# Beacon attention followed by a gated feed-forward block: queries in blocks that line up with the key tiles, whole-batch DMA transposes, and the fourth result pair turned by DMA

## The chip, the cores and the metric

The kernel runs on one core of a Trainium2 chip. The metric is the device time of one execution in microseconds (us). Where a profile is read, PE is TensorE (matmuls; PEld its weight loads), DVE is VectorE, ACT is ScalarE, POOL is GpSimd and SP is SyncE, which here only issues DMAs. A "q" behind an engine (SPq) is its instruction queue.

## The reference: what is computed

```python
# q, k, v: (8, 8, 576, 64); beacon_k, beacon_v: (8, 8, 16, 64)
k_all = np.concatenate([beacon_k, k], axis=2)          # 592 keys
v_all = np.concatenate([beacon_v, v], axis=2)
scores = scale * np.matmul(q, k_all.transpose(0, 1, 3, 2))
causal[:, Nb:] = np.triu(np.ones((S, S), dtype=bool), k=1)   # beacons are seen by all
scores = np.where(causal, -1e9, scores)
a = softmax(scores)
attn = np.matmul(a, v_all)                             # (8, 8, 576, 64)
x = attn.transpose(0, 2, 1, 3).reshape(4608, 512)
g, val = x @ w_gate, x @ w_val                         # (4608, 1536)
out = (gelu(g) * val) @ w_out                          # (4608, 512), float32
```

## The kernel before

**Two interleaved stages.** There are 8 batches of 576 tokens (attention) and 9 chunks of 512 tokens (feed-forward). In pass `b` of the main loop (L561) the attention of batch `b` is computed head pair by head pair (4 pairs of 2 heads), and between its pieces stand the output matmuls of chunk `b-1`, in portions `o(n)` of n matmuls (48 in all for a chunk). Then the gate and value matmuls of chunk `b` follow (`gv_mms`, `gate_val`): 12 tiles of 128 hidden columns, each with 4 steps `kk` over the 512 model columns. Step `kk` reads the attention result of head pair `kk`. So a pass has an attention stage of some 20 us and a gate and value stage of some 19 us. The order of all instructions is written out by hand (`keep`).

**Attention of a pair.** Scores are computed transposed, keys on partitions: five key tiles of 128, 128, 128, 128 and 80 rows (16 beacons, then 576 keys). Key tile t only meets the queries from `S_LO[t]` on (0, 112, 240, 368, 496), so the query blocks have 112, 128, 128, 128 and 80 (96 with the last) queries and are shifted by 16 against the key tiles. `CHUNKS` packs the score matmuls of a pair into four PSUM pieces of 512, 480, 464 and 208 columns for each head (`scores`, `score_mms`). Two heads use the two halves of TensorE's rows. ACT takes the exponential into `expT`, POOL masks the diagonal blocks (`masks`, L298), PE multiplies with v (`attend`; a column of ones gives the sum), and DVE divides (`normalize`: L334, L336) into `y_sb`.

**Queries and keys are needed transposed** (`qkT`, one buffer: pair, q or k, 640 columns). For batches 0 and 1 TensorE transposes them. For batches 2 to 7 POOL loads q and k (L108), with a conversion from float32 to bf16, into a ring of two buffers, two batches ahead. In the pass before they are used, SP issues ten DMA transposes (`transpose_dma`, L238): five token tiles, q and k in turn, each with 4 blocks of at most 128x128.

**Results are needed transposed** too (`xT_sb`, the feed-forward input). For b of 1 to 7 pairs 0, 1 and 2 are turned by two DMA transposes each on SP's queue (`turn_dma`, L368: the first 112 rows, then four tiles). Pair 3 is turned by TensorE: five transposes (`turn`, `tr`, L180) into PSUM in the midst of the output matmuls, and a DVE copy (`put`, L386). The first two tiles of gate and value run their steps in the order pair 0, 3, 1, 2.

**What stands on the queues at the start of the gate and value stage** (L622 to L630): SP stores what is left of the outputs; POOL waits in `hold` (L378) until pair 2 has landed in `xT_sb`, and then issues the loads of v for batch b+1 and of q and k for batch b+2; SP issues the ten transposes for batch b+1. Each chunk has four output stores of 128 rows. Two are issued by ACT in the attention stage (L582, L597) and two by SP, one at L609 and one at L623.

Of the kernel before, what the change touches and what calls it, by code (L numbers as in the profile page):

```python
# [7 lines left out]
P = 128  # L8
B, H, S, NB, D = 8, 8, 576, 16, 64
SK = S + NB  # L10
N_TOK = B * S
# [9 lines left out]

S_LO = [0, 112, 240, 368, 496]
KROWS = [128, 128, 128, 128, 80]
DIAG = [112, 128, 128, 128, 80]


CHUNKS = [
    [(0, 0, 512, 0)],
    [(0, 512, 64, 0), (2, 240, 336, 64), (4, 496, 80, 400)],
    [(1, 112, 464, 0)],  # L30
    [(3, 368, 208, 0)],
]
CHUNK_W = [512, 480, 464, 208]
CHUNK_OFF = [0, 512, 992, 1456]
EXP_W = 1664

EXP_OFF = [0, 992, 576, 1456, 912]
DV = D + 1

Q_N = [128, 128, 128, 128, 80]  # L40
QK_SCALE = 0.125
# [10 lines left out]
def kernel(  # L52
# [16 lines left out]
    ring = ctx.enter_context(tc.tile_pool(name="ring", bufs=1))  # L69
    npool = ctx.enter_context(tc.tile_pool(name="npool", bufs=4))  # L70
    fpool = ctx.enter_context(tc.tile_pool(name="fpool", bufs=3))
    hpool = ctx.enter_context(tc.tile_pool(name="hpool", bufs=2))
# [12 lines left out]
    wo_sb = const.tile([P, F_TILES, D_MODEL], BF16, name="wo_sb", tag="wo_sb")  # L85
    xT_sb = const.tile([P, NPAIR, N_TOK + P - Q_N[4]], BF16, name="xT_sb", tag="xT_sb")

    exp_ring = ring.tile([P, NPAIR, 2, EXP_W + P - Q_N[4]], BF16, name="expT", tag="expT")
    nc.vector.memset(exp_ring[:, :, :, EXP_W:], 0.0)

# [10 lines left out]

    qkT = ring.tile([P, NPAIR, 2, 640], BF16, name="qkT", tag="qkT")
    nc.vector.memset(qkT[:, :, 1, SK:640], 0.0)

    neg = const.tile([P, 256], BF16, name="neg", tag="neg")
# [6 lines left out]
    def qk6_of(b):  # L112
        if b not in qk6:
            qk6[b] = (
                hpool.tile([P, 2, H, 6 * D], BF16, name="qk6", tag="hT_sb"),
                npool.tile([NB, H, D], BF16, name="kb", tag="kb"),
            )
        return qk6[b]
# [12 lines left out]
    def key_loads(src, beacon, dst, b):  # L131
        parts = [
            (dst[0:NB, 0, :, :], beacon[b].rearrange("h t d -> t h d")),
            (dst[NB:P, 0, :, :], src[b, :, 0:112, :].rearrange("h p d -> p h d")),
        ]
        for j in range(1, 5):
            n = KROWS[j]
            r0 = 112 + (j - 1) * P
            parts.append((dst[0:n, j, :, :], src[b, :, r0 : r0 + n, :].rearrange("h p d -> p h d")))
        return [lambda o=o, i=i: dma(o, i) for o, i in parts]  # L140

    def qk_loads(b):
        q_sb, k_sb = q_ring[b % NRING], k_ring[b % NRING]
        parts = []
        for j in range(5):
            n = P if j < 4 else 64
            parts.append(
                (q_sb[0:n, j, :, :], q[b, :, j * P : j * P + n, :].rearrange("h p d -> p h d"))
            )
        return [lambda o=o, i=i: dma(o, i) for o, i in parts] + key_loads(k, beacon_k, k_sb, b)  # L150

# [81 lines left out]
    def transpose_dma(b):  # L233
        q_sb, k_sb = q_ring[b % NRING], k_ring[b % NRING]
        for j in range(5):
            for w, src, n, c in ((0, q_sb, P if j < 4 else 64, NB), (1, k_sb, P if j < 4 else 80, 0)):
                keep(
                    nc.sync.dma_start_transpose(  # L238
                        out=qkT[:, :, w, c + j * P : c + j * P + n],
                        in_=src[0:n, j, :, :].rearrange("p h d -> p (h d)"),  # L240
                    )
                )

    def scores(b, *parts):
# [17 lines left out]
    def score_mms(b, m, c, s_ps):  # L262
        for t, s_lo, w, col in CHUNKS[c]:
            diag = b == 0 and s_lo == S_LO[t]
            for hi in range(2):
                r = slice(64 * hi, 64 * hi + 64)
                mm(
                    s_ps[:, hi, col : col + w],
                    qkT[r, m, 1, t * P : (t + 1) * P],
                    qkT[r, m, 0, NB + s_lo : NB + s_lo + w],  # L270
                    True,
                    not diag,
                    skip_group_check=True,
                )
            if diag:
                base, n = (NB if t == 0 else 0), DIAG[t]
                for k0, width in ((0, min(n, 64 - base)), (64, n)):
                    for hi in range(2):
                        r = slice(64 * hi, 64 * hi + 64)
                        c0 = 64 + 64 * hi - k0  # L280
                        mm(
                            s_ps[:, hi, col : col + width],
                            eye[r, c0 : c0 + P],
                            neg[r, c0 + base : c0 + base + width],
                            False,
                            k0 == 64,
                            skip_group_check=True,
                        )

    def masks(b, m, c):  # L290
        expT = exp_ring[:, m, :, :]
        for t, s_lo, _, _ in CHUNKS[c]:
            if s_lo != S_LO[t]:
                continue
            n = DIAG[t]
            d = expT[0 : KROWS[t], :, EXP_OFF[t] : EXP_OFF[t] + n]
            keep(
                nc.gpsimd.affine_select(  # L298
                    out=d,
                    in_=d,  # L300
                    pattern=[[0, 2], [1, n]],
                    compare_op=ALU.is_ge,
                    fill=0.0,
                    base=NB if t == 0 else 0,
                    channel_multiplier=-1,
                )
            )

    x_of = {}

    def attend(b, m, hi, x_ps):
        expT, v_sb = exp_ring[:, m, :, :], v_ring[b % NRING]
        for j in range(5):
            for t in range(j + 1):
                e0 = EXP_OFF[t] + S_LO[j] - S_LO[t]
                mm(
# [10 lines left out]
    def normalize(b, m, x_ps, h0, h1):  # L327
        i = b * NPAIR + m
        if h0 == 0:
            y_of[i] = npool.tile([P, 5, 2, D], BF16, name="y_sb", tag="y_sb")  # L330
        r_sb = npool.tile([P, 2, 5, 1], FP32, name="r_sb", tag="r_sb")
# [18 lines left out]
    def av_head(b, m, hi, pool, tag):  # L350
        x = pool.tile([P, 1, 512], FP32, name="x_ps", tag=tag)
        attend(b, m, hi, x[:, 0, :])
        normalize(b, m, x, hi, hi + 1)

    def turn(b, m, pool=None, tag="t"):
        y_sb = y_of[b * NPAIR + m].rearrange("p j e d -> p j (e d)")
        y_ps = (pool or psum_t).tile([P, 1024], BF16, name="y_ps", tag=tag)
        y_of[b * NPAIR + m] = y_ps
        for j in range(5):
            n = Q_N[j] if j else S_LO[1]  # L360
            tr(y_ps[:, S_LO[j] : S_LO[j] + n], y_sb[0:n, j, :])

    def turn_dma(b, m):
        y_sb = y_of.pop(b * NPAIR + m)
        n0 = b * S
        for n, j0, j1, q0 in ((S_LO[1], 0, 1, 0), (P, 1, 5, S_LO[1])):
            keep(
                nc.sync.dma_start_transpose(  # L368
                    out=xT_sb[:, m, n0 + q0 : n0 + q0 + n * (j1 - j0)].rearrange("p (j n) -> p j n", n=n),
                    in_=y_sb[0:n, j0:j1, :, :].rearrange("p j e d -> p (j e d)"),  # L370
                )
            )

    hold_sb = const.tile([P, 2], BF16, name="hold_sb", tag="hold_sb")
# [5 lines left out]
    def put(b, m, by_act=False):  # L380
        y_ps = y_of.pop(b * NPAIR + m)
        out_ap = xT_sb[:, m, b * S : (b + 1) * S]
        if by_act:
            act(out_ap, y_ps[:, 0:S], ACT.Copy)
        else:
            keep(nc.vector.tensor_copy(out_ap, y_ps[:, 0:S]))  # L386

# [173 lines left out]
    for b in range(B):  # L561
# [6 lines left out]
        if b:  # L568
# [12 lines left out]
            scores(b, (1, 2))  # L581
            store(nc.scalar)  # L582
            ahead(2)
# [12 lines left out]
            scores(b, (3, 0))  # L596
            store(nc.scalar)  # L597
            av_head(b, 1, 0, psum_o, "o")
# [8 lines left out]
            av(b, 3)  # L607
            o(7)
            store(nc.sync)  # L609
            turn(b, 3)  # L610
            put(b, 3)
            o(4)
            keep(nc.scalar.preload_act_table_set(SET_GELU))
            for kk in (0, 3, 1, 2):
                for fi in range(2):
                    gv_mms(b, fi, kk, last=kk == 2)
        for fi in range(F_TILES):
# [4 lines left out]
            if fi == 0:  # L622
                store(nc.sync)  # L623
                if b and b + 1 < B:
                    hold(b, 2)
                    load_v(b + 1)
                if b and b + 2 < B:
                    load_qk(b + 2)
                if 2 <= b + 1 < B:
                    transpose_dma(b + 1)  # L630
    for fi in range(F_TILES):
        gate_val(N_CHUNKS - 1, fi)
        out_mms(N_CHUNKS - 2, 4 * fi, 4 * fi + 4)
# [37 lines left out]
```

## Time and profile before

Six runs of the kernel have a median of 369.24 us (368.76 to 370.71).

| what | value |
|---|---|
| the profiled execution's own time | 370.71 us |
| its span in the profile | 369.0 us |
| PE busy | 358.9 us, 97% of the span, 3018 matmuls |
| DVE, ACT, POOL busy | 152.5 (41%), 188.2 (51%), 160.5 us (43%) |
| gate and value matmuls (both kinds, 795 recorded) | 110.9 + 110.9 us |
| output matmuls | 101.7 us |
| score matmuls x384; matmuls with v x960 | 34.1 us; 37.1 us |
| POOL's loads and SP's transposes and stores, packets | 104848 on q0; 48000 on q1 |

The profile's page gives busy time of each engine, the chain of work that ended last, and groups of instructions. Durations of single matmuls are latencies (they overlap); what one costs in a row of matmuls is the distance from start to start. Of SP the profile shows only issues; the time of a transfer is that from the issue to the landing of its last byte's semaphore. Some matmul records are missing: about every 10.8 us one start is left out, which looks like a gap of 0.05 us and is none.

### The profile page before, as it was taken

How to read it: one execution, taken by the hardware profiler on the slowest of the kernel's cores; microseconds unless marked ns; L12 is line 12 of the kernel's file. 1: busy time of each engine (PE TensorE's matmuls, PEld its weight loads, DVE VectorE, ACT ScalarE, POOL GpSimd, SP SyncE). 2: the span in 40 equal slices, each digit the busy share in tenths (PEclk: the TensorE clock that was granted, in tenths of full speed). 3: DMA queues.
4: the chain of work that ended last, by engine and by line, in shares of the span. 5: the costliest groups of instructions: out<-in, count | busy, mean ns of one | idle time of the engine just before them, and what ended most of it. 6: DMA issues, size and time to landing. Idle time of an engine off the chain costs nothing.

```text
span 369.0 us, 7507 instructions
## 1 busy us (share of the span) xinstructions
PE 358.9 (97%) x3018; PEld 184.2 (50%) x3061; DVE 152.5 (41%) x277; ACT 188.2 (51%) x243; POOL 160.5 (43%) x288
## 2 busy tenths in 40 slices
PE   7899999999999999999999999999999999999996
PEld 7674546444554446444644454445544464444443
DVE  3454545433344335343533254434444253334332
ACT  3873489136933594339723792369344953331210
POOL 8934478383548252953476353936230430000000
PEclk9899999999999999999999999999999999999999
DMA  7999999799249954999399925992395051000112
GB/s 107 176 203 204 193 121 120 135 147 136 74 111 147 135 61 107 153 143 91 69 159 134 121 63 123 156 138 74 105 132 56 31 81 58 0 2 29 57 37 108
DMA packets 154900, 39.65 MB, mean 107 GB/s; under 512 B 141424, under 2 KB 150384, under 8 KB 154864
## 3 DMA queue, kind: packets, MB, share of 16 engines
q0 software_dynamic: 104848, 19.11, 67.9%
q1 hardware_dynamic: 48000, 16.38, 26.2%
q10 hardware_dynamic: 2016, 3.67, 3.1%
q8 instruction: 24, 0.39, 0.4%
q14 instruction: 12, 0.10, 0.1%
HBM read 38.27 MB, written 9.44 MB: 129 GB/s over the span
## 4 chain that ended last, share of the span: by engine, by line
PE 76%; DMA 12%; SPq 4%; POOL 2%; issue 2%; DVE 2%; ACT 1%; POOLq 0%; DVEq 0%
PE gv_ps L172 32%; PE o_ps L172 23%; PE x_ps L172 9%; PE s_ps L172 8%; DMA qkT<-k_sb 7%; DMA q_sb<-in_q_dram 4%; SPq L238 3%; PE t_ps L180 2%; POOL v_sb L108 2%; DMA xT_sb<-y_sb 1%; PE w_ps L172 1%; PE v_ps L172 1%; ACT expT L175 1%; PE g_ps L172 1%; PE y_ps L180 1%
## 5 line engine op out<-in xcount | busy, mean ns | idle before, releaser
L175 ACT ACTIVATE ge_sb<-gv_ps 128x512 bf16<-128x512 f32 x101 | 59.4, 597 | 144.5 <-PE gv_ps L172 142.6
L427 DVE TENSOR_TENSOR hT_sb<-gv_ps,ge_sb 128x512 bf16<-128x512 f32 x101 | 69.1, 691 | 115.5 <-ACT ge_sb L175 113.1
L172 PE MATMUL gv_ps<-xT_sb,wg_sb 128*128 128x512 bf16 x394 | 110.9, 379 | 0.5
L172 PE MATMUL gv_ps<-xT_sb,wv_sb 128*128 128x512 bf16 x401 | 110.9, 379 | 0.1
L175 ACT ACTIVATE expT<-s_ps 128x960 bf16<-128x960 f32 (+3 forms) x112 | 99.8, 966 | 9.3 <-PE s_ps L172 8.4
L172 PE MATMUL o_ps<-wo_sb,hT_sb 128*128 128x512 bf16 (+2 forms) x415 | 101.7, 373 | 1.4 <-issue 0.2
L298 POOL TENSOR_SCALAR_AFFINE_SELECT expT<-expT 128x256 bf16<-128x256 bf16 (+2 forms) x140 | 51.5, 385 | 67.6 <-ACT expT L175 66.8
L172 PEld LDWEIGHTS <-wv_sb 128*128 128x128 bf16 x432 | 42.3, 98 | 50.4
L172 PEld LDWEIGHTS <-wg_sb 128*128 128x128 bf16 x432 | 42.0, 98 | 50.4 <-DMA xT_sb<-y_sb 0.6
L172 PEld LDWEIGHTS <-hT_sb 128*128 128x128 bf16 x444 | 38.9, 98 | 42.3 <-DVE y_sb L336 3.1
L172 PEld LDWEIGHTS <-expT 128*128 128x128 bf16 (+1 forms) x960 | 33.5, 97 | 10.8 <-DVE y_sb L336 4.1
L172 PE MATMUL s_ps<-qkT 64*128 64x512 bf16 (+5 forms) x384 | 34.1, 285 | 3.5 <-DVE qkT L221 1.0
L172 PE MATMUL x_ps<-v_sb,expT 128*128 128x65 bf16 (+1 forms) x960 | 37.1, 193 | 0.0
L446 DVE COPY o_sb<-o_ps 128x512 f32<-128x512 f32 (+2 forms) x37 | 25.0, 676 | 27.3 <-PE o_ps L172 26.2
L108 POOL DMA_DIRECT2D v_sb<-in_v_dram x40 | 33.6, 858 | 5.9 <-DMA wv_sb<-in_moe_w_val_dram 1.7
L108 POOL DMA_DIRECT2D k_sb<-in_k_dram x30 | 25.2, 843 | 17.8 <-DMA q_sb<-in_q_dram 13.7
L336 DVE TENSOR_TENSOR y_sb<-x_ps,r_sb 128x320 bf16<-128x320 f32 (+1 forms) x47 | 28.8, 612 | 1.6
L334 DVE RECIPROCAL r_sb<-x_ps 128x5 f32<-128x5 f32 (+1 forms) x47 | 9.6, 204 | 47.0 <-PE x_ps L172 47.0
L108 POOL DMA_DIRECT2D q_sb<-in_q_dram x30 | 25.3, 887 | 3.5 <-DMA wo_sb<-in_moe_w_out_dram 3.5
L172 PEld LDWEIGHTS <-qkT 64*128 64x128 bf16 x384 | 14.5, 95 | 19.6 <-issue 12.3
L378 POOL COPY hold_sb<-xT_sb 128x2 bf16<-128x2 bf16 x6 | 1.1, 186 | 33.3 <-DMA xT_sb<-y_sb 33.3
L569 ACT ACT_TABLE_LOAD x7 | 9.0, 1283 | 0.1
(49 smaller groups left out, 122.4 us busy)
## 6 DMA issues: line engine op xcount, KB each, us to landing
out_dram<-o_sb SPq DMA_DIRECT2D x21, 256.0 KB, 2.2
out_dram<-o_sb ACTq DMA_DIRECT2D x14, 256.0 KB, 2.7
v_sb<-in_v_dram POOLq DMA_DIRECT2D x24, 128.0 KB, 6.3
q_sb<-in_q_dram POOLq DMA_DIRECT2D x24, 128.0 KB, 8.1
k_sb<-in_k_dram POOLq DMA_DIRECT2D x18, 128.0 KB, 7.8
wo_sb<-in_moe_w_out_dram POOLq DMA_DIRECT2D x3, 512.0 KB, 14.4
wg_sb<-in_moe_w_gate_dram POOLq DMA_DIRECT2D x2, 512.0 KB, 11.3
wv_sb<-in_moe_w_val_dram POOLq DMA_DIRECT2D x2, 512.0 KB, 12.6
```

Source lines behind the costliest of these rows:

```text
L108: keep(nc.gpsimd.dma_start(out=out_ap, in_=in_ap))
L172: keep(nc.tensor.matmul(out_ap, lhsT, rhs, start=start, stop=stop, **kw))
L175: keep(nc.scalar.activation(out_ap, in_ap, func, **kw))
L180: keep(nc.tensor.transpose(out_ap, in_ap, ident[0:n, 0:n]))
L238: nc.sync.dma_start_transpose(out=qkT[:, :, w, c + j * P : c + j * P + n], in_=src[0:n, j, :, :].rearrange("p h d -> p (h d)"),)
L298: nc.gpsimd.affine_select(out=d, in_=d, pattern=[[0, 2], [1, n]], compare_op=ALU.is_ge, fill=0.0, base=NB if t == 0 else 0, channel_multip ...
L334: keep(nc.vector.reciprocal(r, x[:, :, :, D:DV]))
L336: nc.vector.tensor_tensor(out=y_of[i][:, :, h0:h1, :].rearrange("p j b d -> p b j d"), in0=x[:, :, :, 0:D], in1=r.to_broadcast([P, h1 - h0 ...
L378: keep(nc.gpsimd.tensor_copy(hold_sb, x[:, 0 : S : S - 1]))
L427: nc.vector.tensor_tensor(out=h_of[ci][:, fi, :], in0=gv_of.pop((ci, fi))[1], in1=ge_sb, op=ALU.mult)
L446: keep(nc.vector.tensor_copy(o_sb[:, ti, c0:c1], o_ps))
L569: keep(nc.scalar.preload_act_table_set(SET_EXP))
```

## The change

1. **Query blocks line up with key tiles.** 16 empty columns stand ahead of the queries (as the 16 beacons stand ahead of the keys), so `LO` is 0, 128, 256, 384, 512, and the pieces are 512, 496, 464 and 208 columns wide.
2. **One DMA transpose for all q and one for all k of a batch**, 20 blocks of 128x128 each, in place of ten. The layout of `qkT` for these batches (2 to 7) is by token tile (`qkT_by_tile`). A score matmul that runs from the first four tiles into the fifth is cut in two at column 512: three more pairs of matmuls for each head pair. Batches 0 and 1 keep the old layout and their uncut matmuls.
3. **One DMA for each result pair**: 5 blocks, in place of 1 and 4. Since the blocks are shifted by 16 rows now, DVE first copies the last 16 rows of the batch before into the first 16 rows of `y_sb` (its pool gets 6 buffers).
4. **Pair 3 is turned by DMA as well**: five TensorE transposes and the DVE copy go, in each of batches 1 to 7. The first two gate and value tiles take the pairs in the order 0, 1, 2, 3.
5. **Stores last**: the four stores of a chunk are issued by SP, behind the transposes for the next batch; none by ACT. `hold` waits for pair 3.
6. Seven more DVE clears at the start, for the padding.

```diff
-S_LO = [0, 112, 240, 368, 496]
+LO = [0, 128, 256, 384, 512]
...
-    [(0, 512, 64, 0), (2, 240, 336, 64), (4, 496, 80, 400)],
-    [(1, 112, 464, 0)],
-    [(3, 368, 208, 0)],
+    [(0, 512, 80, 0), (2, 256, 336, 80), (4, 512, 80, 416)],
+    [(1, 128, 464, 0)],
+    [(3, 384, 208, 0)],
...
-    qkT = ring.tile([P, NPAIR, 2, 640], BF16, name="qkT", tag="qkT")
+    qkT_sb = ring.tile([P, NPAIR * 2 * 640], BF16, name="qkT", tag="qkT")
+    qkT = qkT_sb.rearrange("p (m w c) -> p m w c", m=NPAIR, w=2)
+    qkT_by_tile = qkT_sb.rearrange("p (w j m c) -> p w j m c", w=2, j=5, m=NPAIR)
     nc.vector.memset(qkT[:, :, 1, SK:640], 0.0)
+    nc.vector.memset(qkT[:, :, 0, 0:NB], 0.0)
+
+    for r in range(NRING):
+        nc.vector.memset(q_ring[r][0:32, 0, :, :], 0.0)
+        nc.vector.memset(q_ring[r][64:P, 4, :, :], 0.0)
+        nc.vector.memset(k_ring[r][64:P, 4, :, :], 0.0)
...
     def transpose_dma(b):
...
+        for w, ring_w in ((0, q_ring), (1, k_ring)):
+            keep(
+                nc.sync.dma_start_transpose(
+                    out=qkT_by_tile[:, w].rearrange("p j m c -> p (j m) c"),
+                    in_=ring_w[b % NRING].rearrange("p j h d -> p (j h d)"),
                 )
+            )
...
+            if b < 2:
+                pieces = [(lo, lo + w)]
+            else:
+                pieces = [(c0, c1) for c0, c1 in ((lo, min(lo + w, 512)), (max(lo, 512), lo + w)) if c0 < c1]
+            for c0, c1 in pieces:
+                for hi in range(2):
...
+                    elif c0 < 512:
+                        k_ap, q_ap = qkT_by_tile[r, 1, t, m, :], qkT_by_tile[r, 0, c0 // P : c1 // P, m, :]
+                        o_ap = o_ap.rearrange("p (j c) -> p j c", c=P)
+                    else:
+                        k_ap, q_ap = qkT_by_tile[r, 1, t, m, :], qkT_by_tile[r, 0, 4, m, 0 : c1 - c0]
+                    mm(o_ap, k_ap, q_ap, True, not diag, skip_group_check=True)
...
     def turn_dma(b, m):
-        y_sb = y_of.pop(b * NPAIR + m)
-        n0 = b * S
-        for n, j0, j1, q0 in ((S_LO[1], 0, 1, 0), (P, 1, 5, S_LO[1])):
-            keep(
-                nc.sync.dma_start_transpose(
-                    out=xT_sb[:, m, n0 + q0 : n0 + q0 + n * (j1 - j0)].rearrange("p (j n) -> p j n", n=n),
-                    in_=y_sb[0:n, j0:j1, :, :].rearrange("p j e d -> p (j e d)"),
-                )
-            )
+        y_sb, y_before = y_of[b * NPAIR + m], y_of.pop((b - 1) * NPAIR + m)
+        keep(nc.vector.tensor_copy(y_sb[0:NB, 0, :, :], y_before[KROWS[4] - NB : KROWS[4], 4, :, :]))
+        c0 = b * S - NB
+        keep(
+            nc.sync.dma_start_transpose(
+                out=xT_sb[:, m, c0 : c0 + 5 * P].rearrange("p (j n) -> p j n", n=P),
+                in_=y_sb.rearrange("p j e d -> p (j e d)"),
+            )
+        )
...
-            store(nc.scalar)
...
-            store(nc.scalar)
...
             av(b, 3)
-            o(7)
-            store(nc.sync)
-            turn(b, 3)
-            put(b, 3)
-            o(4)
+            turn_dma(b, 3)
+            o(11)
             keep(nc.scalar.preload_act_table_set(SET_GELU))
-            for kk in (0, 3, 1, 2):
+            for kk in range(K_CHUNKS):
                 for fi in range(2):
-                    gv_mms(b, fi, kk, last=kk == 2)
+                    gv_mms(b, fi, kk, last=kk == 3)
...
             if fi == 0:
-                store(nc.sync)
                 if b and b + 1 < B:
-                    hold(b, 2)
+                    hold(b, 3)
                     load_v(b + 1)
                 if b and b + 2 < B:
                     load_qk(b + 2)
                 if 2 <= b + 1 < B:
                     transpose_dma(b + 1)
+                store(nc.sync)
```

## The prediction

> **What bounds the kernel now.** I read the page first: busy shares, then the chain that ended last.
>
> ```profile
> PE 358.9 (97%) x3018; PEld 184.2 (50%) x3061; DVE 152.5 (41%) x277; ACT 188.2 (51%) x243; POOL 160.5 (43%) x288
> ...
> PE 76%; DMA 12%; SPq 4%; POOL 2%; issue 2%; DVE 2%; ACT 1%; POOLq 0%; DVEq 0%
> ```
>
> PE is the bound, everywhere: no other engine passes 51%. The chain's 12% of DMA only says that some releases come from transfers, not that PE stood still for them. So I went through PE's timeline, here around the start of pass 5 and the end of its attention stage.
>
> ```profile
> 206.70 0.76 PE L172 MATMUL s_ps<-qkT 64*128 64x512 bf16 x8
> 207.79 0.21 PE L172 MATMUL s_ps<-qkT 64*128 64x80 bf16 x2 [0.33 <-DMA qkT<-k_sb]
> ...
> 223.62 0.42 PE L180 MATMUL y_ps<-eye,y_sb 112*128 112x112 bf16 x5
> 223.88 0.38 PE L172 MATMUL o_ps<-wo_sb,hT_sb 128*128 128x512 bf16 x1
> ```
>
> Columns are start, length, instruction; in brackets the idle time before. The scores stand still once, for k's last DMA transpose. Pair 3's five transposes hold PE from 223.62 to 223.88. The third view is SP's queue for the same stage, the fourth POOL's.
>
> ```profile
> 221.80 2.49 SPq L368 DMA_TRANSPOSE xT_sb<-y_sb  x2
> 224.38 1.61 SPq L454 DMA_DIRECT2D out_dram<-o_sb  x2
> 226.10 1.28 SPq L238 DMA_TRANSPOSE qkT<-q_sb  x1
> 227.48 1.21 SPq L238 DMA_TRANSPOSE qkT<-k_sb  x1
> ...
> 238.60 1.22 SPq L238 DMA_TRANSPOSE qkT<-k_sb  x1
> ```
>
> ```profile
> 227.52 0.18 POOL L378 COPY hold_sb<-xT_sb 128x2 bf16<-128x2 bf16 x1 [6.33 <-DMA xT_sb<-y_sb]
> 228.01 0.53 POOL L108 DMA_DIRECT2D v_sb<-in_beacon_v_dram  x1 [0.30 <-issue]
> ```
>
> ```profile
> DMA to landing us min/median/max: 2.9/6.7/7.6
> ```
>
> SP spends about 1.3 us on each of ten transposes, and they land 2.9 to 7.6 us after issue (last line: qkT, window 206 to 250); the last at 245.5, one microsecond before the next pass begins at 246.5. In the pass shown above it landed at 207.7, after the start.
>
> **The change part by part**, against the profiled execution (370.71 us, span 369.0).
>
> *Pair 3 off PE.* Five transposes cost 223.88 - 223.62 = 0.26 us of PE, with no idle time around them. Seven batches: -1.83 us. DVE's copy (0.46 us) goes too; DVE is not late, so nothing.
>
> *When does pair 3 land instead?* Pass 5: the last matmul with v starts at 222.08, DVE's product ends at 223.38 (L336, 0.82 us). The 16-row copy is not in the trace; the nearest row, 128x16 from PSUM, is 0.16 us. SP issues at 223.6. In the trace one block takes SP 1.12 us and four 1.26, so five take 1.3; they landed 2.2 and 2.5 us after issue when undisturbed, so five in 2.6: 226.2. PE needs them after eleven output matmuls (11 x 0.216) and twelve of gate and value (12 x 0.216), from 222.11: 227.1. The allowance from issue to landing is 3.45 us, so 0.9 us to spare. The trace warns: pair 2's last DMA took 4.0 to 4.3 us in passes 1, 3, 5 and 7, 2.5 in the others. In those four a single 16,384-byte packet of queue q8 (the page's "instruction": 24) began 1.1 to 2.3 us after the issue. 24 packets and 6161 PE instructions are one packet per 256; in the trace most began when PE had issued 178 to 211 of its 256. Counting the changed program's instructions, that place falls into the critical stretch in pass 1, at its edge in pass 6, else not. Cost from 0 to 7 x 0.75; taken: +0.4 for pass 1.
>
> *One DMA for q, one for k.* SP reaches q at 225.0 (before: 226.1), since pair 3 takes 1.3 us of issue, and stores and pair 2's second DMA are gone from ahead of it. At 0.046 us a block (1.26 - 1.12 over three), 20 blocks cost SP 2.0 us, both 4, instead of 13. The rows are 5120 of 256 bytes instead of 4672. In the packet records transposes run at 800 a us alone and 410 a us beside POOL's loads, in bursts of one DMA, with 0.7 to 1 us between bursts. Alone until 229.6, q takes 3.2 us; k beside the loads 6.3 us and about 1.6 to land: some 239, against 246.3 needed. Waits on these transposes in the trace, start to start beyond the columns: 0.49 us (pass 5), 0.23 (pass 3), 0.09 on pair 2: up to -0.8. The profiled execution is the slowest of the runs, so the median may hold less; -0.4 from the median. From the other side: if blocks are paced as the ten DMAs were (2.06 us for each 512 rows), k lands near 247.5; that is a rival. I take the burst, since within a DMA of four blocks no pause shows.
>
> *Scores.* 24 more matmuls a batch for six batches. A rule speaks against it: the Trainium skill, "TensorE: Matmul & The Clock Gate", section "Back-to-back issue gap", gives sustained pairs of weight load and matmul about 81 ns at 128 columns. Priced so, 24 x 81 ns less the 12 x 33 ns of columns taken over is 1.5 us a batch, +9 us in all. The trace has the case itself: pairs of 80 columns are followed 32 to 36 ns later by the next pair, 464 columns cost 193, 336 cost 140, 208 cost 87, which is columns/2.4 with nothing added; the two heads start 3 to 4 ns apart. 384 + 80 is then 160 + 33 = 193, as before. I take the rows: 0; ends 0 and 4 ns a pair (+0.3). A moving operand in blocks 512 elements apart is nowhere in the trace; all here are contiguous; I take 0, as each block is itself 128 contiguous elements, a gain has no reason, and 10 ns a block would be +2. Sixteen more columns in one piece: 64 to 80 costs nothing visible on PE (35 against 32 ns) and 0.03 us on ACT (0.9 ns a column of 32). In the middle of the stage PE waits 0.15 us for an exponential, so about 0.04 us a batch: +0.3. POOL's mask of 112 becomes 128 wide, 0.38 to 0.41 us, the same +0.03 beside other work.
>
> *Stores last.* Moved behind pair 3, q and k on SP; on ACT two issues of 0.34 us go, hidden there. Nobody waits for them until the output buffer is used again two batches on, so 0. They add about 3 us of DMA after k, while the q transposes have moved ahead of the loads; the loads end about as before (248.1 to 248.6), and POOL's last load issue (243.7) stays clear of its first mask (248.1). If not, masks would be late.
>
> *`hold` on pair 3*: POOL is released at 226.2 instead of 227.4; queued behind it are v (first needed 5 us into the next pass) and q, k a batch later. 0.
>
> *Start.* Seven clears, about 1.6 us of DVE by the 0.14 to 0.22 us of those in the trace; DVE then finishes its mask table near 5.2 instead of 4.9, and is next needed at 5.6. With the wider masks and exponentials of batch 0: +0.1.
>
> *Sum.* From the median: -1.83 - 0.4 + 0.4 + 0.3 + 0.1 = -1.4, so 369.24 - 1.4 = 367.8. From the profiled execution, with -0.8 of waits: 370.71 - 1.8 = 368.9. Runs are spread by 0.5%, and a comparison can tell about 0.3% (1.1 us): faster means below 368.1.
>
> **Rivals.**
> - *The forecast, 0.60*: 367.8, own range 366.7 to 368.6; 0.48 of it is below 368.1.
> - *Gain taken back at the same place, 0.14*: pair 3 is a little late, and PE waits at step 3 what it saved, 0.2 us in each pass: 367.8 + 1.4 = 369.2, no change. For it: 0.9 us of slack is one 16 KB packet. Against: `hold` and so the loads can't begin before pair 3.
> - *Pair 3 clearly late, 0.14*: its landing takes 4.2 us as in four of the seven passes, 0.75 over the allowance of 3.45, in every pass: +5.2 less the 0.4 counted: 372.6, slower. It decides from a mean landing of 3.65 us on.
> - *Whole-batch transposes too late, 0.12*: all of q and k must land before the first score, where before the first score needed only the first tiles' DMAs. Paced as now, k lands at 247.5 against 246.3: 1.2 x 6 = +7.2: 375. Against: SP's issue no longer paces them. Decides from 246.5 on.
>
> **Range and chances.** 366.7 to 372.6 leaves out about 0.2 (the last rival, half of the third and the forecast's tail). Faster 0.50, within 0.3% 0.24, slower 0.26.
>
> **What would show it.** In the changed profile: PE 0.2 us shorter per pass between its last matmul with v and gate and value; ten output matmuls there without a break; k's landing near 239 in pass 5 and no wait for `qkT` at a pass start; SP's two transposes about 2 us each; 80-wide score pairs still near 33 ns apart; pair 3 landing 2.6 us after issue, except in pass 1. I am wrong if gate and value's step 3 waits for `xT_sb` in most passes, if a q or k DMA is busy over 10 us, or if score stages grow by over 0.2 us.

## The result, and the profile after

The changed kernel takes 367.91 us (median of 16 runs, 366.86 to 368.59) against 369.62 us for the kernel before in the same runs (37 runs, 368.76 to 372.36): a ratio of 0.9946, 95% interval 0.9933 to 0.9959, so 1.7 us less by the medians and 2.0 by the ratio. The profiled execution took 368.59 us (370.71 before), its span is 366.8 us (369.0 before). Both lie at the upper end of their kernel's runs, this one as the slowest of its 16.

The page of the changed kernel, busy shares and the chain that ended last:

```profile
PE 356.2 (97%) x3127; PEld 184.2 (50%) x3170; DVE 155.4 (42%) x305; ACT 189.1 (52%) x243; POOL 161.2 (44%) x288
...
PE 94%; DMA 2%; issue 1%; POOL 1%; DVE 1%; POOLq 0%
```

PE is still the bound and is 2.7 us less busy, with 109 more matmuls: 24 x 6 cut pieces more, 7 x 5 transposes fewer. The chain now runs through PE almost alone: 12% of DMA have become 2%.

PE's timeline at the start of pass 5, which showed a gap of 0.33 us before:

```profile
205.59 0.80 PE L173 MATMUL s_ps<-qkT 64*128 64x512 bf16 x14
206.55 1.89 PE L173 MATMUL o_ps<-wo_sb,hT_sb 128*128 128x512 bf16 x8 [0.16 <-issue]
```

All 14 score matmuls stand in one row, and no transfer is waited for. (The 0.16 us behind them is one missing record of an output matmul.) The same view at the end of this pass's attention:

```profile
220.69 2.54 PE L173 MATMUL o_ps<-wo_sb,hT_sb 128*128 128x512 bf16 x11
223.06 0.38 PE L173 MATMUL gv_ps<-xT_sb,wg_sb 128*128 128x512 bf16 x1
...
225.65 0.38 PE L173 MATMUL gv_ps<-xT_sb,wg_sb 128*128 128x512 bf16 x1
225.87 0.38 PE L173 MATMUL gv_ps<-xT_sb,wv_sb 128*128 128x512 bf16 x1
```

The eleven output matmuls are unbroken, and so are gate and value behind them. The one at 225.65 is the first of step 3, which reads pair 3. SP's queue in this stage:

```profile
219.94 3.50 SPq L372 DMA_TRANSPOSE xT_sb<-y_sb  x2
223.68 3.12 SPq L237 DMA_TRANSPOSE qkT<-q_sb  x1
227.02 5.13 SPq L237 DMA_TRANSPOSE qkT<-k_sb  x1
232.21 2.14 SPq L458 DMA_DIRECT2D out_dram<-o_sb  x4
```

Pair 3 is the second of the first line: issued at 222.25, landed at 224.82, 0.83 us ahead of its reader. And who waits for the transposes, from the answers for the tiles `xT_sb` (whole run) and `qkT` (window 206 to 250):

```profile
L372 SPq DMA_TRANSPOSE xT_sb<-y_sb x28: 1199/1200/1813, 57.7 to 300.6; - x28
...
who waited for it (us, times):
  POOL hold_sb L382: 31.0, 6
...
DMA to landing us min/median/max: 2.5/2.6/4.5
```

```profile
L237 SPq DMA_TRANSPOSE qkT<-k_sb x1: 5131/5131/5131, 227.0 to 227.0; - x1
...
who waited for it (us, times):
busy tenths in 40 slices 0000000000000000000000000000000000000000
DMA to landing us min/median/max: 6.8/8.9/11.1
```

Only POOL's `hold`, which is there to wait, waits for the results; nobody for q and k. k takes the 11.1 us: issued at 227.02, landed at 238.1; the next pass begins at 244.74.

**Where the time went.** From the first score of one pass to that of the next:

| pass | 1 | 2 | 3 | 4 | 5 | 6 |
|---|---|---|---|---|---|---|
| before, us | 40.26 | 39.32 | 39.46 | 39.32 | 39.82 | 39.32 |
| after, us | 40.07 | 39.16 | 39.16 | 39.16 | 39.15 | 39.16 |

The passes sum to 237.50 us before and 235.85 after: 1.65 less. In passes 3 and 5 the waits for k (0.14 and 0.50 over the other passes) are gone; apart from them passes 2 to 6 are 0.16 shorter each, and pass 1 is 0.19 shorter. Of the rest of the 2.2 us of span, 0.29 lies ahead of pass 1, where first loads arrive, and about 0.3 behind pass 6.

### The profile page after: what moved, and what is told of

Same layout as the page of the kernel before. It is cut to its first block, busy times and chain, and to the rows that moved or that the text cites. A ratio compares the mean times of both kernels' runs of the same rounds, so it can differ in the third digit from the quotient of the medians.

```text
span 366.8 us, 7625 instructions
## 1 busy us (share of the span) xinstructions
PE 356.2 (97%) x3127; PEld 184.2 (50%) x3170; DVE 155.4 (42%) x305; ACT 189.1 (52%) x243; POOL 161.2 (44%) x288
## 4 chain that ended last, share of the span: by engine, by line
PE 94%; DMA 2%; issue 1%; POOL 1%; DVE 1%; POOLq 0%
PE gv_ps L173 47%; PE o_ps L173 25%; PE x_ps L173 9%; PE s_ps L173 8%; DMA qk<-in_q_dram 2%; PE v_ps L173 2%; PE g_ps L173 2%; PE t_ps L181 1%; POOL qk L116 1%; PE y_ps L181 0%; DVE qkT L200 0%; DVE qkT L218 0%; DVE qkT L204 0%; POOL eye L485 0%; DVE o_sb L450 0%
## 5 line engine op out<-in xcount | busy, mean ns | idle before, releaser
L173 PE MATMUL gv_ps<-xT_sb,wv_sb 128*128 128x512 bf16 x388 | 107.9, 379 | 0.4
L176 ACT ACTIVATE expT<-s_ps 128x992 bf16<-128x992 f32 (+3 forms) x112 | 100.7, 972 | 9.3 <-PE s_ps L173 9.0
L173 PE MATMUL o_ps<-wo_sb,hT_sb 128*128 128x512 bf16 (+2 forms) x420 | 100.6, 373 | 2.1 <-issue 1.1
L303 POOL TENSOR_SCALAR_AFFINE_SELECT expT<-expT 128x256 bf16<-128x256 bf16 (+1 forms) x140 | 52.4, 390 | 55.6 <-ACT expT L176 54.2
L173 PE MATMUL s_ps<-qkT 64*128 64x80 bf16 (+5 forms) x528 | 34.6, 254 | 1.7 <-ACT qkT L176 0.7
L339 DVE TENSOR_TENSOR y_sb<-x_ps,r_sb 128x320 bf16<-128x320 f32 (+1 forms) x47 | 28.8, 612 | 1.6
L173 PEld LDWEIGHTS <-qkT 64*128 64x128 bf16 x528 | 17.1, 96 | 18.2 <-issue 12.2
## 6 DMA issues: line engine op xcount, KB each, us to landing
wo_sb<-in_moe_w_out_dram POOLq DMA_DIRECT2D x3, 512.0 KB, 14.4
```

Source lines behind the costliest of these rows:

```text
L173: keep(nc.tensor.matmul(out_ap, lhsT, rhs, start=start, stop=stop, **kw))
L176: keep(nc.scalar.activation(out_ap, in_ap, func, **kw))
L303: nc.gpsimd.affine_select(out=d, in_=d, pattern=[[0, 2], [1, n]], compare_op=ALU.is_ge, fill=0.0, base=0, channel_multiplier=-1,)
L339: nc.vector.tensor_tensor(out=y_of[i][:, :, h0:h1, :].rearrange("p j b d -> p b j d"), in0=x[:, :, :, 0:D], in1=r.to_broadcast([P, h1 - h0 ...
```

## The experiments

Theory A: the gain is pair 3's place on PE (0.26 us a pass) and the end of the waits for q and k; it stands because pair 3 lands less than 1 us ahead of its reader. Rivals: the gain comes from the other parts (one DMA for q and k, the place of the stores), and pair 3 brings nothing; or the cuts and widths of the scores cost something that hides a larger gain. The kernel before, run beside them, had medians of 369.56 to 369.85 us. None of these kernels leaves out any of the computation.

| edit | median us | ratio to before (95%) | passes 2 to 6, us |
|---|---|---|---|
| the change | 367.91 | 0.9946 (0.9933 to 0.9959) | 39.15 to 39.16 |
| pair 3 on TensorE | 369.45 | 0.9986 (0.9964 to 1.0007) | 39.41 to 39.42 |
| pair 3's step second | 374.21 | 1.0103 (1.0068 to 1.0138) | 40.07 to 40.13 |
| ten transposes, no cuts | 368.03 | 0.9944 (0.9921 to 0.9967) | 39.14 to 39.15 |
| ten transposes, cuts | 367.47 | 0.9929 (0.9902 to 0.9956) | 39.15 to 39.16 |
| a cut at every 128 columns | 367.68 | 0.9933 (0.991 to 0.9957) | 39.18 to 39.19 |
| stores ahead, as before | 367.57 | 0.9929 (0.9906 to 0.9953) | 39.15 to 39.16 |
| ten transposes and stores ahead | 371.66 | 1.0056 (1.0039 to 1.0073) | 39.25 to 40.54 |
| every pair by two DMAs | 378.5 | 1.023 (1.0204 to 1.0255) | 40.46 to 41.54 |
| only pair 3 by two | 369.9 | 1.0 (0.9982 to 1.0017) | 39.45 to 39.50 |
| pairs 0, 1, 2 by two | 371.3 | 1.0052 (1.0033 to 1.0071) | 39.29 to 40.12 |
| before, and pair 3 by two DMAs | 384.96 | 1.0398 (1.0361 to 1.0434) | 40.87 to 43.23 |
| one output matmul later | 366.15 | 0.9905 (0.9883 to 0.9928) | 38.94 |

**Pair 3 back on TensorE.** The changed kernel, with this part undone:

```diff
-            turn_dma(b, 3)
-            o(11)
+            o(7)
+            turn(b, 3)
+            put(b, 3)
+            o(4)
...
-            for kk in range(K_CHUNKS):
+            for kk in (0, 3, 1, 2):
...
-                    hold(b, 3)
+                    hold(b, 2)
```

> The changed kernel with pair 3 turned by TensorE again (five transposes and the DVE copy, step order 0, 3, 1, 2, hold on pair 2). Theory A (the gain is TensorE time: 0.26 us in each of seven passes): 1.8 us slower than the changed kernel, so about 369.7 us, ratio to the kernel before 1.000, and the passes 0.26 us longer than the changed kernel's 39.16. Rival B (the gain is the waits on q's and k's transposes, and pair 3 by DMA is taken back elsewhere): stays near 368, ratio 0.995.

369.45 us. Each pass is 0.26 us longer (39.42 against 39.16), just what five transposes cost PE. With everything else of the change in place the kernel can't be told from the one before. So pair 3 is the part that pays. The other parts about cancel: there is no wait for k any more, but a pass takes 39.42 us, where an undisturbed one of the kernel before takes 39.32.

**Pair 3's step second, as before.** It takes away the cover under which the transfer lands:

```diff
-            for kk in range(K_CHUNKS):
+            for kk in (0, 3, 1, 2):
                 for fi in range(2):
-                    gv_mms(b, fi, kk, last=kk == 3)
+                    gv_mms(b, fi, kk, last=kk == 2)
```

> The changed kernel with only the step order of the first two gate and value tiles set back to 0, 3, 1, 2, so that pair 3 is needed 8 matmuls (1.73 us) earlier. Pair 3 lands 2.57 us after its issue in the changed kernel's profile; the allowance of 3.45 us falls to 1.72. Theory A (pair 3 is hidden only by standing last, with 0.9 us to spare): TensorE waits 0.85 us in each of seven passes, +6.0 us, about 373.9, ratio 1.012, and the wait shows on gate and value's second step. Rival (pair 3's landing is well hidden anyway): no change, ratio 0.995.

374.21 us. Its answer for `xT_sb` has a new line under who waited, and its PE timeline in pass 5 the gap:

```profile
  PE gv_ps L173: 6.9, 7
...
DMA to landing us min/median/max: 2.6/2.6/4.3
```

```profile
226.28 0.38 PE L173 MATMUL gv_ps<-xT_sb,wg_sb 128*128 128x512 bf16 x1
227.65 0.38 PE L173 MATMUL gv_ps<-xT_sb,wg_sb 128*128 128x512 bf16 x1 [0.98 <-DMA xT_sb<-y_sb]
```

The transfer takes the same 2.6 us, but its reader comes eight matmuls (8 x 0.216 = 1.7 us) sooner, and PE stands still for the 0.9 us that the slack doesn't cover, in every pass. The order of the steps, which reads as a detail of the diff, decides between faster and slower.

**Ten transposes for q and k, without and with the cuts.** Two kernels: one with the old layout of `qkT`, ten DMAs and uncut scores, and one with ten DMAs into the layout by token tile, cut:

```diff
-        for w, ring_w in ((0, q_ring), (1, k_ring)):
-            keep(
-                nc.sync.dma_start_transpose(
-                    out=qkT_by_tile[:, w].rearrange("p j m c -> p (j m) c"),
-                    in_=ring_w[b % NRING].rearrange("p j h d -> p (j h d)"),
...
+        for j in range(5):
+            for w, ring_w in ((0, q_ring), (1, k_ring)):
+                keep(
+                    nc.sync.dma_start_transpose(
+                        out=qkT_by_tile[:, w, j],
+                        in_=ring_w[b % NRING][:, j, :, :].rearrange("p h d -> p (h d)"),
```

The "rule of 81 ns" in these expectations and in the next is the one that the prediction cites and doubts.

> The changed kernel with ten DMA transposes again for q and k (128 rows each, padded), into the layout of before (by pair), and the score matmuls uncut. Theory A (whole-batch transposes remove the waits at a pass's start, worth 0.4 us in a median run, and the cuts cost 0.1 us a pass, 0.6 in all): within 0.5 us of the changed kernel, 367.5 to 368.3, with passes 0.05 to 0.1 us shorter where no wait falls. Rival C (the two whole-batch DMAs are what gains): back to about 369.5. k's last transpose lands near 245 in pass 5 instead of 238.

> The changed kernel with ten DMA transposes for q and k into the new layout by token tile, score matmuls cut as in the changed kernel. Against e3_ten_uncut it gives the price of the cuts alone: theory A 0.05 to 0.1 us a pass, 0.3 to 0.6 us in all; by the rule of 81 ns a small matmul it would be 9 us. Against the changed kernel it gives the price of ten DMAs in place of two: 0 to 0.8 us of waits by theory A, over 1.5 us by rival C.

368.03 and 367.47 us, passes of 39.14 to 39.16: neither the one DMA for each of q and k nor the cuts move the time. In the cut kernel the last of ten lands at 243.38, 0.5 us ahead of the pass (243.87), where one DMA each lands 6.7 us ahead. The wide margin buys nothing as long as the stores stand last.

**A cut at every 128 columns.** It multiplies the suspected cost:

```diff
-                pieces = [(c0, c1) for c0, c1 in ((lo, min(lo + w, 512)), (max(lo, 512), lo + w)) if c0 < c1]
+                pieces = [(c0, min(c0 + P, lo + w)) for c0 in range(lo, lo + w, P)]
```

> The changed kernel with every score matmul of batches 2 to 7 cut at each 128 columns: 6 more cuts for each head and pair, 48 more matmuls (and weight loads) a pass, 288 in all. By the rows (time is columns/2.4, nothing for a cut): no change, 367.9, at most 0.1 us a pass. By the rule of 81 ns for a matmul of 128 columns with its weight load, where the columns take 53: from 1.3 us a pass (28 ns on each of 48) upwards, 8 us in all, 376.

367.68 us with 282 more matmuls on record (3409 against 3127): 0.02 to 0.03 us a pass for 48 matmuls. At these sizes cuts are as good as free.

**Stores ahead, as before**, first with one DMA each for q and k, then with ten:

```diff
             scores(b, (1, 2))
+            store(nc.scalar)
...
             scores(b, (3, 0))
+            store(nc.scalar)
...
-            o(11)
+            o(7)
+            store(nc.sync)
+            o(4)
...
             if fi == 0:
+                store(nc.sync)
...
                     transpose_dma(b + 1)
-                store(nc.sync)
```

> The changed kernel with the four stores of a chunk where they were: two on ACT's queue in the attention stage, two on SP's ahead of the transposes. Theory A: q's transpose starts some 1 to 1.5 us later, k's still lands 6 us before the pass that needs it: no change, 367.9, ratio 0.995. Rival (the stores' place took the waits away): waits return, +0.4 to 0.8 us.

> The changed kernel with ten DMA transposes for q and k (as before, in the layout by token tile) and the stores placed as before (two issued by ACT, two by SP ahead of the transposes). Ten transposes with the stores last showed no wait at all, though the kernel before, with ten, showed 0.49, 0.23 and 0.09 us. Theory S (it is SP's reach of the transposes that took the waits away: no stores and no second DMA of pair 2 ahead of them): the last one lands near 245 to 245.5 in the frame of pass 5 against a start at 243.9 to 244.7, waits of 0.1 to 0.5 us come back in two or three passes: 368.2 to 369. Rival L (the loads' places or the layout took them away): no wait, 367.6.

367.57 us with one DMA each: nothing. With ten 371.66 us, some 4 us more than ten transposes with the stores last, and more than theory S said. The start of pass 6, ten transposes with stores last, then with stores ahead:

```profile
243.87 0.81 PE L173 MATMUL s_ps<-qkT 64*128 64x512 bf16 x14
244.83 1.89 PE L173 MATMUL o_ps<-wo_sb,hT_sb 128*128 128x512 bf16 x8 [0.16 <-issue]
```

```profile
245.82 0.77 PE L173 MATMUL s_ps<-qkT 64*128 64x512 bf16 x12
247.91 0.21 PE L173 MATMUL s_ps<-qkT 64*128 64x80 bf16 x2 [1.32 <-DMA qkT<-k_sb]
```

In the second the last transpose lands at 247.87, and PE has waited for it. Five passes are 0.1 to 1.4 us longer than 39.16, 3.8 us in sum. So the waits of the kernel before are held off by either of two parts, stores last or one DMA each, and come back only when both are undone. Why they are so much longer here than in the kernel before is open: from the first issue to the last landing ten transposes took 22.1 us here, 19.4 in the kernel before and 20.7 with the stores last. The padded blocks have 5120 rows for 4672, and the loads beside them start at other times; neither was tried alone.

**Two DMAs for each pair**, with aligned blocks, and the kernel before with nothing but pair 3 moved to two DMAs:

```diff
+        for j0, j1 in ((0, 1), (1, 5)):
...
-                out=xT_sb[:, m, c0 : c0 + 5 * P].rearrange("p (j n) -> p j n", n=P),
-                in_=y_sb.rearrange("p j e d -> p (j e d)"),
+                    out=xT_sb[:, m, c0 + j0 * P : c0 + j1 * P].rearrange("p (j n) -> p j n", n=P),
+                    in_=y_sb[:, j0:j1, :, :].rearrange("p j e d -> p (j e d)"),
```

```diff
             av(b, 3)
+            turn_dma(b, 3)
             o(7)
             store(nc.sync)
-            turn(b, 3)
-            put(b, 3)
             o(4)
...
-            for kk in (0, 3, 1, 2):
+            for kk in range(K_CHUNKS):
...
-                    hold(b, 2)
+                    hold(b, 3)
```

> The changed kernel with each result pair turned by two DMAs (one block, then four) in place of one of five. SP takes 2.4 us a pair instead of 1.2. In the changed kernel's pass 5 pair 2 is issued at 219.94 and pair 3 at 222.25, so pair 3's second DMA is issued at 223.5 to 223.6 and lands at 226.1, where step 3 begins at 225.7. Theory A: a wait of 0.3 to 0.4 us a pass, +2.1 to 2.8 us against the changed kernel, 370 to 370.7, ratio 1.001 to 1.003. Rival (issue time is hidden): no change, 367.9.

> The kernel before with pair 3 alone changed: turned by DMA as the other pairs are, by two DMAs, step order 0, 1, 2, 3, hold on pair 3. In pass 5 of the kernel before SP is busy with pair 2 until 224.3; pair 3's two issues end at 226.8 and its second DMA, issued at 225.5, lands at 228.0, where step 3 begins at 227.1. Theory A (pair 3 by DMA pays only because each pair takes one issue): 0.9 us of wait in each pass less the 0.26 saved, +4.5 us against the kernel before, 374, ratio 1.012. Rival (moving pair 3 alone is the change's whole gain): 368, ratio 0.995.

378.5 and 384.96 us: the direction was right, the sizes were not (some 8 us and 11 us short). The SP view of the first in pass 5 and its answer for `xT_sb` show what the expectation left out:

```profile
219.82 12.54 SPq L373 DMA_TRANSPOSE xT_sb<-y_sb  x8
232.59 3.06 SPq L237 DMA_TRANSPOSE qkT<-q_sb  x1
```

```profile
  PE gv_ps L173: 9.3, 8
```

The first line groups all four pairs; after pair 0 SP idles until 224.23, and from pair 1 on it issues without a pause. Two issues take some 2.6 us, but the pairs come 1.9 and 2.3 us apart (the issues of the changed kernel: 218.04, 219.94, 222.25), so SP falls behind by the pair. The last DMA of pair 3 landed at 233.57, 9.34 us after pair 1's first issue (224.23). In the changed kernel pair 3 lands 6.78 after it, and its reader comes 7.61 after it. 9.34 - 7.61 = 1.73 late; PE's step 3 came 1.70 us late. The expectation had priced pair 3's own two issues and not the queue ahead of them. In the second kernel the same happens (first line below, from its answer for `xT_sb`), and the ten transposes behind start later too (the others, from that for `qkT`):

```profile
  PE gv_ps L172: 10.4, 8
```

```profile
  PE s_ps L172: 2.6, 5
  PEld L172: 2.4, 3
```

**Which of the pairs?** The same edit for pair 3 alone (`if m == 3`), and for the other three alone:

> The changed kernel with only pair 3 turned by two DMAs (1 and 4 blocks); pairs 0 to 2 by one each. It tells whether two DMAs for one pair are dear by themselves, or only with those of the pairs ahead of them on SP's queue. Theory Q (queue): in the changed kernel pair 3 is issued at 222.25 in pass 5, lands at 224.82 and is needed at 225.65. In two, the second is issued 1.2 us later and lands 2.5 after that, at 225.9: 0.25 us late, in each of seven passes, +1.8: 369.7 us. Rival D (two DMAs are dear by themselves, by what all four pairs in two cost, 1.5 us a pass): 378.

> The changed kernel with pairs 0, 1 and 2 by two DMAs each and pair 3 by one. Theory Q: pairs 1 and 2 hold SP for four issues of 1.25 to 1.35 us from 218.04 on, so pair 3 is issued near 223.3 in place of 222.25 and lands near 225.9 against 225.65: 0.25 us a pass; where pair 2's second DMA lands 4.2 us after its issue (three passes) up to 1 us more. +1.8 to +4: 369.7 to 372. Together with the case in which only pair 3 is in two, it makes the 1.5 us a pass of all four pairs in two. Rival D (the cost lies in pair 3's own second DMA): 368, as the changed kernel.

369.9 and 371.3 us, both much as theory Q has it: 0.3 us a pass for pair 3 alone (0.8 in pass 1), 0.1 to 1.0 for the others. Together they would be some 5 us; both at once cost 10.6. The price is in the queue that builds up, not in a DMA by itself. "One DMA for each pair" is therefore no ornament beside "pair 3 by DMA": without it pair 3 by DMA is a loss.

**One output matmul later.** The waits left in a pass of the changed kernel are two of 0.11 and 0.17 us in the middle of the attention stage. A trial to shift one matmul under them:

```diff
             scores(b, (1, 2))
             ahead(2)
-            o(6)
+            o(5)
             av_head(b, 0, 0, psum_t, "t")
...
             turn_dma(b, 0)
-            o(6)
+            o(7)
```

> The changed kernel with one output matmul moved: o(6) becomes o(5) ahead of the first head of pair 0, and the o(6) behind pair 0's transpose becomes o(7). PE waits about 0.1 us a pass for DVE's copy of the score transposes' successor in that bank and for exponentials in the middle of the stage. If a matmul placed there covers a wait: up to -0.1 us a pass, 367.1. If the wait only moves: 367.6 to 367.9, as the changed kernel. If the first head then waits for its own exponential: up to +0.1 us a pass, 368.5.

366.15 us, 0.9905 (0.9883 to 0.9928): the best version of all, each pass 0.22 us shorter (38.94). The first wait is for a PSUM bank: the third output tile uses the bank from which DVE still divides pair 0's second head (L339). PE's weight loads, the changed kernel, then this one:

```profile
174.28 0.11 PEld L173 LDWEIGHTS <-hT_sb 128*128 128x128 bf16 x2 [0.44 <-DVE y_sb L339]
```

```profile
172.27 0.21 PEld L173 LDWEIGHTS <-hT_sb 128*128 128x128 bf16 x2 [0.22 <-DVE y_sb L339]
```

The weight load waits half as long, and the matmul behind it no longer (0.11 us beyond its columns before, none now). The second wait is that of a 512-column score matmul for an exponential, 8.97 us into the pass. The exponential now comes 0.22 us earlier in the pass, since the scores that it reads stand ahead of the moved matmul; the score matmul is ready only 0.10 us earlier, and the wait falls from 0.17 to 0.05 us. One edit covers most of both, twice what was expected. The kernel before has the same two waits (0.11 and 0.16 us); the edit was not tried there.

## Why the prediction was right, point by point

- *Pair 3 off PE, -0.26 a pass*: right; undoing it gives back 0.26 a pass and 1.5 us in all.
- *Pair 3 lands 2.6 us after issue, 0.9 us to spare*: right, 2.55 to 2.65 in all seven passes, and 0.75 to 0.87 to spare. The rival in which PE waits at step 3 what it saved didn't come; the run with the step second shows what it hung on: with 1.7 us of cover taken away PE waited 0.9 us.
- *+0.4 for pair 3 late in pass 1*: wrong. It landed 2.57 us after issue there too. Late landings (4.1 to 4.5 us) did occur, but on pair 0 in pass 1 and pair 2 in passes 1, 3 and 6, where the reader comes later. In the packet records of the changed kernel these four are just the transfers for which a 16,384-byte instruction packet began 0.8 to 2.1 us after the issue, as the prediction had read it; in pass 1 the packet began at 65.5 us, 0.05 ahead of pair 3's issue, and did no harm. So the danger was real and only its place was wrong: counting instructions (6161 by the prediction, 6116 in the trace) did not place a packet to within the microsecond that mattered. That none met pair 3 in seven passes is luck.
- *q at 2.0 us of SP, k too*: mis-sized. SP took 3.1 us for q and 4.7 to 5.4 for k. The extrapolation from one block to four blocks did not hold for 20. It did no harm: nothing but stores stands behind, and k landed 14.4 us after q's issue (223.7 to 238.1 in pass 5), where 14 was predicted (225 to 239). The rival in which k comes too late for the pass had 22.5 and was off by 8 us: the blocks of one DMA are not paced like ten DMAs. The packet records show 778 to 849 rows a us from 225 to 228, while no load ran; 800 was taken. The sign of being wrong, a DMA busy over 10 us, is met only if k's 11.1 to 11.7 us from issue to landing are read so: in pass 5 its own rows ran for 5 of them, from 230 to 235, behind q's.
- *Waits for q and k, -0.4*: the waits went, 0.64 us in this pair of profiles (what they cost in a median run is not known). But the cause was named too narrowly. The prediction credited one DMA each; the runs show that stores last does it as well.
- *Stores last, 0*: right as the change stands, and wrong as a general price: with ten transposes the place of the stores is worth 4 us.
- *Cuts, 0*: right, against the rule of the Trainium skill's page "TensorE: Matmul & The Clock Gate", section "Back-to-back issue gap", that by the prediction's estimate would have made +9 us of them. Two kernels show it: uncut is no faster, and 282 more matmuls are no slower. At these sizes the measured rows decide.
- *Sixteen more columns, +0.04 a batch*: mis-sized, +0.10 a pass between the first score and gate and value (the last output matmuls begin 15.10 us into the pass, 15.01 before). In pass 4 0.01 to 0.02 us of it comes with each of the five groups of scores, and 0.03 in the last matmuls with v, where a wait grows from 0.03 to 0.06 us. The uncut kernel has the same passes to 0.01 us, so it isn't the cuts. Sixteen columns at 2.4 a ns are 7 ns, less than what a group shows; the width alone was not undone, and the rest of its cost is open.
- *The sum*: 369.24 - 1.4 = 367.8 was predicted, 367.91 measured. The difference to the kernel before was -1.7 by the medians, as that kernel's own median over more runs is 369.62. With measured terms: -1.83 (pair 3), -0.64 (waits), +0.7 (7 x 0.10, widths), +0.1 (start, left as estimated) = -1.67. Against the prediction's -1.4 two errors cancel: 0.4 for a late pair 3 that never came, and 0.4 that the widths cost beyond their estimate. So the main term and its mechanism were right, and that the sum came within 0.1 us is partly luck.

## What to carry to other kernels

When work is moved from the bound engine to a DMA, sum the queue ahead of the new transfer (issues by arrival times, not the transfer's own price alone), and set its landing against its reader's place in the instruction order: here 0.8 us of slack decided, and both "one DMA a pair" and the order of the steps were conditions of the gain. Two edits that each remove the same wait show nothing when undone singly; undo them together before calling either worthless. And look for the last small waits of the bound engine in a repeated stage: here moving one matmul by a few lines gave as much again (1.8 us) as the whole change.

## What the runs showed of the hardware that was not expected

- A DMA transpose of 5 blocks holds SP 1.20 us and lands 2.6 us after issue; the same blocks as 1 and 4 hold it 1.12 + 1.26 us. The second DMA costs an issue, not a landing. In the changed kernel one of 20 blocks holds SP 3.1 us, and a second directly behind it 4.7 to 5.4 us.
- PE loses some 95 to 107 ns, start to start beyond the columns, at nearly every change between full-height matmuls and the half-height scores, before and after alike: in the changed kernel a 512-column output matmul at 171.79 is followed by a score at 172.10, 0.31 us, where an output matmul follows another after 0.216. With about ten such changes a pass this is near 1 us a pass; what it is was not tested.
- Cutting the moving operands of the scores at every 128 columns (48 more matmuls a pass) costs under 0.03 us a pass.
- A transpose of a result pair that meets an instruction packet, begun 0.8 to 2.1 us after its issue, lands 4.1 to 4.5 us after the issue in place of 2.6 (four of 28 in the changed kernel; this rests on the coincidence of the two in time, packets were not moved on purpose).
